# A fused attention and two-layer feed-forward kernel: the first token block takes its weights in two parts, with the second block between them

## The chip, the cores and the metric

The kernel runs on one core of a Trainium2 chip. The metric is device time in microseconds of one execution; the median over the runs is compared. Engines are called as in the profile: PE (matrix products; PEld its weight loads), DVE (vector), ACT (scalar), POOL, and SP, whose queue issues the DMAs. Each engine works through its own instructions in order.

## What is computed

```python
# r, k, v, w: (4, 8, 768, 48); attention is a recurrence over the sequence
cur = einsum('bhd,bhe->bhde', u * k[t], v[t])
y[t] = einsum('bhd,bhde->bhe', r[t], state + cur)
state = w[t][..., None] * state + einsum('bhd,bhe->bhde', k[t], v[t])
# then two feed-forward layers over 3072 tokens, 384 -> 2048 -> 384 each
h = x @ w_in;  g = where(h >= 1, h, where(h <= -1, 0, (h + 1)**2 / 4));  x = g @ w_out
h = x @ w2_in; g = where(h > 0, h, exp(min(h, 0)) - 1);                  out = g @ w2_out
```

The feed-forward weights arrive as 64-bit floats; the kernel converts them to 32 bits itself.

## The kernel before, in words

Attention is done in 24 steps (`attention`, stages of `QuotientAttention.stages`), each for 128 tokens. The 3072 tokens form six blocks of 512, four steps each. A block and a layer make a job: jobs 0 to 5 are the first layer on blocks 0 to 5, jobs 6 to 11 the second layer. A job runs 16 slots, one for each 128 hidden units, f = 0 to 15. A slot (job, f) is gemm1 (line 172, nine matmuls of 512 columns; operands are split in a high and a low part, so three products replace one), the activation (`first`, `second`; lines 183 to 192), the split of its result (`split`, 217 on ACT and 218 on DVE) and gemm2 (line 227, nine matmuls, which add into three PSUM banks y over all 16 slots; the first six need ACT's half of the split only). After slot 15 `store_y` copies y out (line 234 on ACT) and stores it.

Weight f (`weight_stages`) is loaded (111), taken apart on ACT (118, 119), converted on DVE (125 to 130: `last`), and cut in high and low part by ACT (135) and DVE (136: `parts`). The 16 weights of the first layer stay in SBUF for all its jobs, in `wpool` (line 75); raw weights of the first half are loaded into places that later hold weights of the second half, raw weights 10 and 12 into the second buffer of x (`RAW_X`).

An attention step has seven stages: `decays` (438 to 442, DVE), `operands`, `scores`, `masked` (479), `placed`, `out`, `stored`. Steps 0 to 3 write x of block 0 straight to SBUF (`x_act`, 425 and 426); the others store to DRAM (`out_act`, 343), from where `load_x` (158) and `split_x` (164, 165) fetch the block's x one job ahead.

The order of the work is written out by hand: `at(tick, rank, fn)` files each piece under a tick, and at the end (798 to 800) all pieces are emitted by tick and rank. Slot (ji, f) starts at tick t0 + 16 ji + f, with gemm1 at this tick, activation one tick later, the split two and gemm2 three ticks later; t0 is 20. `START` and `AT1` place the attention steps of blocks 0 and 1, `AT` those of the later blocks, `WSTART` the weights; `RANK_W`, `RANK_A` and `RANK_S` order the pieces within a tick. In block 0 weight f is due at tick t0 + f, so one weight for each slot (line 782). The framework may move a piece a little ahead where an engine would else stand idle. While steps 0 to 3 run, idle matmuls on zeros (`warm`, 151) are put on PE.

After block 5's attention `swap` frees its buffers, a second set of y banks is opened and the second layer's weights are converted (lines 791 to 797).

Of the kernel before, what the change touches and what calls it, by code (L numbers as in the profile page):

```python
# [9 lines left out]
F32 = mybir.dt.float32  # L10
F32R = mybir.dt.float32r
I32 = mybir.dt.int32
# [17 lines left out]
NB = max(BLOCKS) * TS  # L30


START = [0, 4, 8, 12]
AT1 = [-4, 0, 3, 7]
AT = [-6, 0, 4, 7]
T0 = 2
WSTART = [15, 16, 18, 24, 25, 27, 23, 23, 27, 34, 29, 35, 34, 36, 40, 45]
W2, W2_STEP = 4, 1.65
W_AHEAD, X_AHEAD, X_SPLIT = 1, 2, 1

RANK_W = [[148, 62, -48], [96, 102, -10]]
RANK_A = [[80, 126, 173, 72, 35, 21, 37], [72, 103, 199, 65, -3, 0, 8]]
RANK_S = [[-12, 45, 56, 52, -26], [-15, 37, 46, 56, -7]]

ON_ACT = {0: 0b0110101101101101, 5: 0b1111111011111101, 6: 0b1000100000011110}
TOK_POOL = {(6, 1), (7, 1), (7, 2), (6, 0)} | {(s, 2) for s in range(8, NSTEP)}
RAW_X = [10, 12]
NMORE = 5

WARM = [[3, 3, 3, 3, 3, 3, 3], [1, 2, 0, 3, 2, 2, 2], [2, 1, 4, 3, 4, 1, 2], [3, 2, 2, 1, 2, 3, 2]]  # L50
# [13 lines left out]
class Moe:  # L64


    def __init__(self, tc, ctx):
        self.tc, self.nc = tc, tc.nc
        nc = self.nc

        def pool(name, bufs, **kw):
            return ctx.enter_context(tc.tile_pool(name=name, bufs=bufs, **kw))

        const = pool("const", 1)
        self.wpool = [pool("wpool0", NF // 2), pool("wpool1", NF // 2)]
        self.xp = pool("xp", 2)
        self.ep = pool("ep", 2)
        self.gp = pool("gp", 2)
        self.ph = pool("ph", 2, space=PSUM)
        self.py = [pool("py", 1, space=PSUM)]  # L80
        self.one = const.tile([P, 1], F32, name="one")
        nc.gpsimd.memset(self.one, 1.0)
        self.half = const.tile([P, 1], F32, name="half")
        nc.gpsimd.memset(self.half, 0.5)
        self.zero = const.tile([P, P], mybir.dt.bfloat16, name="zero")
        nc.gpsimd.memset(self.zero, 0.0)
# [4 lines left out]

    def place(self, f):

        return self.wpool[f // (NF // 2)], "w"

    def new_raw(self, pool=None, tag="w_raw"):
        return (pool or self.wraw).tile([P, 2 * DM, 2], I32, name="w_raw", tag=tag)
# [52 lines left out]
        for _ in range(n):  # L150
            self.nc.tensor.matmul(y, self.zero, free_ap(self.zero, 0, P, 0, [[0, 512]]), start=True, stop=True)

    def new_x(self):
        return self.xp.tile([P, 2, 3, NB], F32R, name="x_hl")

    def load_x(self, src, t0, n):
        x = self.new_x()
        self.nc.sync.dma_start(x[:, 1, :, :n].bitcast(F32), src.rearrange("(k p) t -> p k t", p=P)[:, :, t0:t0 + n])
        return x

# [66 lines left out]
                self.nc.tensor.matmul(y[d][:, :n], w[:, a, DM + d * P:DM + (d + 1) * P], g[:, b, :n],  # L227
                                      start=first and j == 0, stop=last and j == 2)

    def store_y(self, y, dst, t0, n):  # L230
        nc = self.nc
        for d in range(3):
            o = self.ep.tile([P, NB], F32, name="y_o")
            nc.scalar.copy(o[:, :n], y[d][:, :n])  # L234
            nc.sync.dma_start(dst[d * P:(d + 1) * P, t0:t0 + n], o[:, :n])

    def run(self, jobs, weights):

        for m, src, dst, t, n in jobs:
            x = self.load_x(src, t, n)  # L240
            self.split_x(x, n)
            y = [self.py[0].tile([P, 512], F32, name=f"y{d}") for d in range(3)]
            for f in range(NF):
                h = self.gemm1(weights[(m, f)], x, n)
                first, second, g = self.act1(h, n, False) if m == 0 else self.act2(h, n, False)
                first()
                second()
                self.gemm2(weights[(m, f)], self.split(g, n), y, n, f == 0, f == NF - 1)
            self.store_y(y, dst, t, n)
# [412 lines left out]
def rwkv_moe_moe(ctx: ExitStack, tc: tile.TileContext, io, out):  # L662
# [7 lines left out]
    with ExitStack() as mctx:  # L670
# [12 lines left out]
        xs, ys, hs, gs, weights = {}, {}, {}, {}, {}  # L683

        def raw(m, f):
            if m == 0 and f < NF // 2:
                return moe.new_raw(*moe.place(NF // 2))
            if m == 0 and f in RAW_X:
                if f == RAW_X[0]:
                    xs["raw"] = moe.xp.tile([P, len(RAW_X), 2 * DM, 2], I32, name="x_raw", tag="x_hl")  # L690
                return xs["raw"][:, RAW_X.index(f)]
            return moe.new_raw()

        def weight(tick, m, f, place):
            st = {}
# [33 lines left out]
        def slot(tick, ji, f):  # L729
# [15 lines left out]
                gs[k] = moe.split(hs.pop(k)[2], n)  # L745

            def g2():
                if f == 0 and ji:
                    ys[ji] = [moe.py[ji % len(moe.py)].tile([P, 512], F32, name=f"y{d}") for d in range(3)]
                moe.gemm2(weights[(m, f)], gs.pop(k), ys[ji], n, f == 0, f == NF - 1)  # L750
                if f == NF - 1:
                    moe.store_y(ys.pop(ji), dst, t, n)

            at(tick, RANK_S[int(ji > 0)][0], g1)
            at(tick + 1, RANK_S[int(ji > 0)][1], first)
# [4 lines left out]
        def load_x(tick, ji):  # L760
            _, src, _, t, n = jobs[ji]

            def load():
                xs[ji] = moe.load_x(src, t, n)

            at(tick, 90, load)
            at(tick + X_SPLIT, 65, lambda: moe.split_x(xs[ji], n))
# [9 lines left out]
        for s in range(BLOCKS[0]):  # L777
            attention(START[s], s)
        t0 = START[BLOCKS[0] - 1] + 6 + T0
        at(0, 0, lambda: xs.update({0: moe.new_x()}))  # L780
        for f in range(NF):
            weight(min(WSTART[f], t0 + f - 3), 0, f, lambda f=f: moe.place(f))
        for ji in range(2 * nb):
            for f in range(NF):
                slot(t0 + ji * NF + f, ji, f)
            if ji:
                load_x(t0 + ji * NF - X_AHEAD, ji)
            if ji and ji < nb:
                for i in range(BLOCKS[ji]):
                    attention(t0 + (ji - 1) * NF + (AT1 if ji == 1 else AT)[i], steps[ji] + i)  # L790
        end = t0 + (nb - 2) * NF + AT[-1] + 7
        at(end, 99, swap)
        for f in range(NF):
# [104 lines left out]
```

## Time and profile before

| | us |
|---|---|
| runs | 953.8, 953.16, 948.65 (median 953.16) |
| profiled execution, its own time | 949.87 |
| its span, first to last instruction | 948.1 |
| PE busy | 913.5 (96%) |
| DVE busy | 623.5 (66%) |
| ACT busy | 588.3 (62%) |

Busy time is a mean over stages with different limits. The row of 40 slices shows where an engine is full, and windows of single stretches show how much it stands idle there. Matmuls overlap, so a slot's cost on PE is read from the distance between starts and not from single durations; DVE instructions overlap a little as well.

### The profile page before, as it was taken

The numbers are of one execution on the slowest core, as the hardware profiler recorded it, in microseconds if no ns is written. First come the engines' busy times: TensorE is split into PE (matmuls) and PEld (weight loads), VectorE is DVE, ScalarE is ACT, GpSimd is POOL, SyncE is SP. The second block draws the span as 40 slices with busy tenths as digits, with TensorE's granted clock in tenths as the row PEclk, the third lists the DMA queues.
The fourth block names the chain that finished last, engine by engine and source line by source line (L and its number), as shares of the span: only waits on it lengthen the run. The fifth ranks groups of instructions, "written<-read, shape, count | busy, mean of one in ns | idle before, by whom it ended". The sixth has DMA issues, their size and how long they took to land. (4 is left out here: it accounts for less than half of the span.)

```text
span 948.1 us, 15178 instructions
## 1 busy us (share of the span) xinstructions
PE 913.5 (96%) x5981; PEld 735.1 (78%) x5985; DVE 623.5 (66%) x923; ACT 588.3 (62%) x948; POOL 28.3 (3%) x41
## 2 busy tenths in 40 slices
PE   9787989999999999999999999999999999999996
PEld 4565767788888888888888888888888888888885
DVE  8999899856556755754399995555555545555552
ACT  5798767978878887877699973333433432433322
POOL 1000100000000000000000000000000000000000
PEclk9879999999999999999999999999999999999999
DMA  7876443434233422520274420100100101000001
GB/s 221 303 237 206 141 124 112 132 111 129 69 101 107 129 92 91 159 89 22 55 291 139 165 68 1 34 34 1 55 12 1 67 1 34 34 1 1 34 1 37
DMA packets 41184, 86.25 MB, mean 91 GB/s; under 512 B 5008, under 2 KB 18448, under 8 KB 41104
## 3 DMA queue, kind: packets, MB, share of 16 engines
q1 hardware_dynamic: 41104, 85.20, 27.9%
q8 instruction: 49, 0.80, 0.3%
q14 instruction: 31, 0.25, 0.1%
HBM read 71.81 MB, written 13.37 MB: 90 GB/s over the span
## 5 line engine op out<-in xcount | busy, mean ns | idle before, releaser
L172 PE MATMUL h<-x_hl,w_hl 128*128 128x512 f32 x1728 | 436.8, 397 | 10.9 <-DVE e_g L192 6.4
L227 PE MATMUL y<-g_hl,w_hl 128*128 128x512 f32 x1728 | 427.2, 391 | 4.2 <-DVE g_hl L218 4.2
L172 PEld LDWEIGHTS h<-x_hl,w_hl 128*128 128x128 f32 x1728 | 323.4, 190 | 81.2 <-DVE e_g L192 6.3
L227 PEld LDWEIGHTS y<-g_hl,w_hl 128*128 128x128 f32 x1728 | 324.0, 188 | 72.0 <-DVE g_hl L218 4.8
L218 DVE TENSOR_TENSOR g_hl<-e_g,g_hl 128x512 fp32r<-128x512 f32 x192 | 135.6, 706 | 74.2 <-ACT g_hl L217 73.8
L207 ACT ACTIVATE e_g<-e_g 128x512 f32<-128x512 f32 x90 | 56.9, 632 | 169.2 <-DVE e_g L206 169.2
L217 ACT CAST g_hl<-e_g 128x512 fp32r<-128x512 f32 x192 | 118.5, 617 | 54.0 <-PE y L227 48.6
L210 DVE SCALAR_TENSOR_TENSOR e_g<-e_g,h 128x512 f32<-128x512 f32 x96 | 66.1, 688 | 69.1 <-ACT e_g L207 65.0
L192 DVE TENSOR_TENSOR e_g<-h,e_g 128x512 f32<-128x512 f32 x96 | 65.9, 687 | 59.5 <-ACT e_g L185 59.2
L206 DVE TENSOR_SCALAR e_g<-h 128x512 f32<-128x512 f32 x90 | 62.2, 691 | 56.0 <-PE h L172 55.9
L183 ACT ACTIVATE e_g<-h,half 128x512 f32<-128x512 f32 x88 | 60.3, 685 | 34.7 <-PE h L172 32.0
L184 ACT ACTIVATE e_g<-e_g,one 128x512 f32<-128x512 f32 x88 | 63.8, 725 | 2.2
L185 ACT ACTIVATE e_g<-e_g 128x512 f32<-128x512 f32 x88 | 55.6, 632 | 1.4
L442 DVE TENSOR_TENSOR rk_sb<-rk_sb,w_sb 128x1024 f32<-128x1024 f32 x24 | 29.3, 1222 | 22.1 <-DMA rk_sb<-in_rkq 22.0
L465 PEld LDWEIGHTS sc<-tt,rk_sb 64*64 64x64 f32 x768 | 26.8, 140 | 9.0 <-issue 4.5
L136 DVE TENSOR_TENSOR w_hl<-w_z,w_hl 128x768 fp32r<-128x768 f32 x32 | 30.5, 954 | 3.2 <-ACT w_hl L135 3.1
L234 ACT COPY y_o<-y 128x512 f32<-128x512 f32 x36 | 20.4, 581 | 18.9 <-PE y L227 12.5
L465 PE MATMUL sc<-tt,rk_sb 64*64 64x64 f32 x768 | 31.1, 228 | 1.1 <-ACT tt L310 0.4
L360 PEld LDWEIGHTS ds<-vk_sb,rk_sb 64*64 64x64 f32 x704 | 20.6, 134 | 13.9 <-issue 7.5
L438 DVE TENSOR_TENSOR_SCAN w_sb<-w_sb,start 128x520 f32<-128x520 f32 x24 | 29.7, 1236 | 2.3 <-DMA w_sb<-in_wq 2.3
L441 DVE TENSOR_TENSOR_SCAN w_sb<-w_sb,start 128x520 f32<-128x520 f32 x24 | 30.1, 1256 | 0.5
L135 ACT CAST w_hl<-w_z 128x768 fp32r<-128x768 f32 x32 | 26.6, 832 | 4.8 <-DVE w_z L130 4.7
(68 smaller groups left out, 601.2 us busy)
## 6 DMA issues: line engine op xcount, KB each, us to landing
w_raw<-in_w SPq DMA_DIRECT2D x30, 768.0 KB, 5.1
rk_sb<-in_rkq SPq DMA_DIRECT2D x24, 512.0 KB, 3.9
tok_sb<-in_tokq SPq DMA_DIRECT2D x24, 384.0 KB, 3.1
w_sb<-in_wq SPq DMA_DIRECT2D x24, 260.5 KB, 3.5
x2d<-y_o SPq DMA_DIRECT2D x18, 256.0 KB, 2.2
x_hl<-x2d SPq DMA_DIRECT2D x6, 768.0 KB, 4.5
out_y<-y_o SPq DMA_DIRECT2D x18, 256.0 KB, 2.0
vk_sb<-in_vkq SPq DMA_DIRECT2D x22, 192.0 KB, 4.0
```

The source lines that it names most:

```text
L172: self.nc.tensor.matmul(h[:, :n], w[:, a, k * P:(k + 1) * P], x[:, b, k, :n], start=i == 0, stop=i == 8)
L183: nc.scalar.activation(out=g, in_=h[:, :n], func=AF.Relu, bias=self.half, scale=-0.5)
L184: nc.scalar.activation(out=g, in_=g, func=AF.Relu, bias=self.one, scale=-1.0)
L185: nc.scalar.activation(out=g, in_=g, func=AF.Square)
L192: nc.vector.tensor_tensor(out=g, in0=h[:, :n], in1=g, op=ALU.max)
L206: nc.vector.tensor_scalar_min(g, h[:, :n], 0.0)
L207: nc.scalar.activation(out=g, in_=g, func=AF.Exp)
L210: nc.vector.scalar_tensor_tensor(out=g, in0=g, scalar=1.0, in1=h[:, :n], op0=ALU.subtract, op1=ALU.max)
L217: nc.scalar.copy(gh[:, 0, :n], g)
L218: nc.vector.tensor_tensor(out=gh[:, 1, :n], in0=g, in1=gh[:, 0, :n].bitcast(F32), op=ALU.subtract)
L227: self.nc.tensor.matmul(y[d][:, :n], w[:, a, DM + d * P:DM + (d + 1) * P], g[:, b, :n], start=first and j == 0, stop=last and j == 2)
L465: nc.tensor.matmul(ps[64 * hh:64 * hh + 64, u], c["rk"][q:q + 64, 0, NU - 1 - u], c["tt"][q:q + 64, hh, u], start=True, stop=True)
```

## The change

Block 0 (job 0) runs its slots 0 to 6, then job 1 runs all its 16 slots, then job 0 its slots 7 to 15 (`SPLIT`, `order`). After slot (0,6) y is copied out and stored in the rows of `x2d` that job 0 fills at the end anyway; `load_part` fetches it into a free raw weight buffer near the end of the second part, and after slot (0,15) `store_y` adds it on DVE instead of copying on ACT. The first slot stands at tick 29 instead of 20; the attention steps of block 1 start at ticks 16, 19, 22 and 26, those of block 2 at 37, 42, 46 and 49. Weights follow `WSTART` alone. Every weight place and both x buffers become pools of their own; raw weights 0 to 7, 10 and 11 lie in places of weights 8 to 15. The ranks, and the engine of some activations in jobs 5 and 6 (`ON_ACT`), are set anew.

```diff
@@ -30,21 +30,24 @@
 NB = max(BLOCKS) * TS
 
 
-START = [0, 4, 8, 12]
-AT1 = [-4, 0, 3, 7]
-AT = [-6, 0, 4, 7]
-T0 = 2
-WSTART = [15, 16, 18, 24, 25, 27, 23, 23, 27, 34, 29, 35, 34, 36, 40, 45]
+START = [0, 4, 9, 12]
+AT1 = [-13, -10, -7, -3]
+AT2 = [8, 13, 17, 20]
+AT = [-6, 0, 3, 6]
+T0 = 11
+WSTART = [21, 22, 20, 25, 24, 29, 33, 37, 37, 39, 37, 42, 44, 44, 46, 46]
 W2, W2_STEP = 4, 1.65
+X_POOL = [0, 1, 1] + [ji % 2 ^ 1 for ji in range(3, 12)]
 W_AHEAD, X_AHEAD, X_SPLIT = 1, 2, 1
 
-RANK_W = [[148, 62, -48], [96, 102, -10]]
-RANK_A = [[80, 126, 173, 72, 35, 21, 37], [72, 103, 199, 65, -3, 0, 8]]
-RANK_S = [[-12, 45, 56, 52, -26], [-15, 37, 46, 56, -7]]
-
-ON_ACT = {0: 0b0110101101101101, 5: 0b1111111011111101, 6: 0b1000100000011110}
+RANK_W = [[148, 62, -48], [103, 102, -10]]
+RANK_A = [[80, 146, 173, 72, 35, 21, 85], [39, 103, 199, 65, -3, 0, -18]]
+RANK_S = [[-38, 51, 56, -11, -26], [-4, 37, 46, 56, -7]]
+
+ON_ACT = {0: 27501, 5: 28415, 6: 34836}
 TOK_POOL = {(6, 1), (7, 1), (7, 2), (6, 0)} | {(s, 2) for s in range(8, NSTEP)}
-RAW_X = [10, 12]
+RAW = {f: NF // 2 + f for f in range(NF // 2)} | {10: 14, 11: 15}
+SPLIT = 7
 NMORE = 5
 
 WARM = [[3, 3, 3, 3, 3, 3, 3], [1, 2, 0, 3, 2, 2, 2], [2, 1, 4, 3, 4, 1, 2], [3, 2, 2, 1, 2, 3, 2]]
@@ -72,8 +75,8 @@
             return ctx.enter_context(tc.tile_pool(name=name, bufs=bufs, **kw))
 
         const = pool("const", 1)
-        self.wpool = [pool("wpool0", NF // 2), pool("wpool1", NF // 2)]
-        self.xp = pool("xp", 2)
+        self.wpool = [pool(f"wpool{f}", 1) for f in range(NF)]
+        self.xp = [pool("xp0", 1), pool("xp1", 1)]
         self.ep = pool("ep", 2)
         self.gp = pool("gp", 2)
         self.ph = pool("ph", 2, space=PSUM)
@@ -91,7 +94,7 @@
 
     def place(self, f):
 
-        return self.wpool[f // (NF // 2)], "w"
+        return self.wpool[f], "w"
 
     def new_raw(self, pool=None, tag="w_raw"):
         return (pool or self.wraw).tile([P, 2 * DM, 2], I32, name="w_raw", tag=tag)
@@ -150,11 +153,11 @@
         for _ in range(n):
             self.nc.tensor.matmul(y, self.zero, free_ap(self.zero, 0, P, 0, [[0, 512]]), start=True, stop=True)
 
-    def new_x(self):
-        return self.xp.tile([P, 2, 3, NB], F32R, name="x_hl")
-
-    def load_x(self, src, t0, n):
-        x = self.new_x()
+    def new_x(self, i):
+        return self.xp[i].tile([P, 2, 3, NB], F32R, name="x_hl")
+
+    def load_x(self, src, t0, n, i):
+        x = self.new_x(i)
         self.nc.sync.dma_start(x[:, 1, :, :n].bitcast(F32), src.rearrange("(k p) t -> p k t", p=P)[:, :, t0:t0 + n])
         return x
 
@@ -227,17 +230,20 @@
                 self.nc.tensor.matmul(y[d][:, :n], w[:, a, DM + d * P:DM + (d + 1) * P], g[:, b, :n],
                                       start=first and j == 0, stop=last and j == 2)
 
-    def store_y(self, y, dst, t0, n):
+    def store_y(self, y, dst, t0, n, part=None):
         nc = self.nc
         for d in range(3):
             o = self.ep.tile([P, NB], F32, name="y_o")
-            nc.scalar.copy(o[:, :n], y[d][:, :n])
+            if part is None:
+                nc.scalar.copy(o[:, :n], y[d][:, :n])
+            else:
+                nc.vector.tensor_add(o[:, :n], y[d][:, :n], part[:, d, :n])
             nc.sync.dma_start(dst[d * P:(d + 1) * P, t0:t0 + n], o[:, :n])
 
     def run(self, jobs, weights):
 
-        for m, src, dst, t, n in jobs:
-            x = self.load_x(src, t, n)
+        for i, (m, src, dst, t, n) in enumerate(jobs):
+            x = self.load_x(src, t, n, i % 2)
             self.split_x(x, n)
             y = [self.py[0].tile([P, 512], F32, name=f"y{d}") for d in range(3)]
             for f in range(NF):
@@ -683,13 +689,7 @@
         xs, ys, hs, gs, weights = {}, {}, {}, {}, {}
 
         def raw(m, f):
-            if m == 0 and f < NF // 2:
-                return moe.new_raw(*moe.place(NF // 2))
-            if m == 0 and f in RAW_X:
-                if f == RAW_X[0]:
-                    xs["raw"] = moe.xp.tile([P, len(RAW_X), 2 * DM, 2], I32, name="x_raw", tag="x_hl")
-                return xs["raw"][:, RAW_X.index(f)]
-            return moe.new_raw()
+            return moe.new_raw(*moe.place(RAW[f])) if m == 0 and f in RAW else moe.new_raw()
 
         def weight(tick, m, f, place):
             st = {}
@@ -745,11 +745,12 @@
                 gs[k] = moe.split(hs.pop(k)[2], n)
 
             def g2():
-                if f == 0 and ji:
+                begin, end = f == 0 or k == (0, SPLIT), f == NF - 1 or k == (0, SPLIT - 1)
+                if begin and k != (0, 0):
                     ys[ji] = [moe.py[ji % len(moe.py)].tile([P, 512], F32, name=f"y{d}") for d in range(3)]
-                moe.gemm2(weights[(m, f)], gs.pop(k), ys[ji], n, f == 0, f == NF - 1)
-                if f == NF - 1:
-                    moe.store_y(ys.pop(ji), dst, t, n)
+                moe.gemm2(weights[(m, f)], gs.pop(k), ys[ji], n, begin, end)
+                if end:
+                    moe.store_y(ys.pop(ji), dst, t, n, first_half.get("part") if k == (0, NF - 1) else None)
 
             at(tick, RANK_S[int(ji > 0)][0], g1)
             at(tick + 1, RANK_S[int(ji > 0)][1], first)
@@ -761,7 +762,7 @@
             _, src, _, t, n = jobs[ji]
 
             def load():
-                xs[ji] = moe.load_x(src, t, n)
+                xs[ji] = moe.load_x(src, t, n, X_POOL[ji])
 
             at(tick, 90, load)
             at(tick + X_SPLIT, 65, lambda: moe.split_x(xs[ji], n))
@@ -777,17 +778,30 @@
         for s in range(BLOCKS[0]):
             attention(START[s], s)
         t0 = START[BLOCKS[0] - 1] + 6 + T0
-        at(0, 0, lambda: xs.update({0: moe.new_x()}))
+        at(0, 0, lambda: xs.update({0: moe.new_x(X_POOL[0])}))
+
+
+        def load_part():
+            n = jobs[0][4]
+            p = first_half["part"] = moe.wraw.tile([P, 3, NB], F32, name="y_part", tag="w_raw")
+            nc.sync.dma_start(p[:, :, :n], x2d.rearrange("(k p) t -> p k t", p=P)[:, :, :n])
+
+        order = [(0, f) for f in range(SPLIT)] + [(1, f) for f in range(NF)] + [(0, f) for f in range(SPLIT, NF)]
+        order += [(ji, f) for ji in range(2, 2 * nb) for f in range(NF)]
+        first_half = {}
+        begins = {ji: t0 + order.index((ji, 0)) for ji in range(2 * nb)}
+        at(t0 + 2 * NF, 91, load_part)
         for f in range(NF):
-            weight(min(WSTART[f], t0 + f - 3), 0, f, lambda f=f: moe.place(f))
-        for ji in range(2 * nb):
-            for f in range(NF):
-                slot(t0 + ji * NF + f, ji, f)
-            if ji:
-                load_x(t0 + ji * NF - X_AHEAD, ji)
-            if ji and ji < nb:
+            weight(WSTART[f], 0, f, lambda f=f: moe.place(f))
+        for i, (ji, f) in enumerate(order):
+            slot(t0 + i, ji, f)
+        for ji in range(1, 2 * nb):
+            load_x(begins[ji] - X_AHEAD, ji)
+            if ji < nb:
+                ticks = [t0 + a for a in (AT1 if ji == 1 else AT2)] if ji < 3 else [begins[ji - 1] + a for a in AT]
+                assert ticks[-1] + 6 <= begins[ji] - X_AHEAD and RANK_A[1][6] < 90
                 for i in range(BLOCKS[ji]):
-                    attention(t0 + (ji - 1) * NF + (AT1 if ji == 1 else AT)[i], steps[ji] + i)
+                    attention(ticks[i], steps[ji] + i)
         end = t0 + (nb - 2) * NF + AT[-1] + 7
         at(end, 99, swap)
         for f in range(NF):
```

## Rows read from the trace of the kernel before

**Rows 1.** The page, busy tenths in 40 slices: PE, DVE, granted clock.

```profile
PE   9787989999999999999999999999999999999996
...
DVE  8999899856556755754399995555555545555552
...
PEclk9879999999999999999999999999999999999999
```

**Rows 2.** Windows: busy us (x instructions) of PE, PEld, DVE, ACT, POOL; clock, DMA.

```profile
0.00:66.00 66.00, 53.63 (x758) 34.38 (x762) 59.20 (x93) 46.47 (x76) 3.46 (x20) 0.87 0.79 255
0.00:156.30 156.30, 131.33 (x1355) 92.49 (x1360) 145.24 (x222) 119.93 (x190) 10.76 (x25) 0.91 0.62 203
4.30:151.10 146.80, 122.90 (x1299) 87.13 (x1301) 139.08 (x213) 113.02 (x180) 8.09 (x9) 0.91 0.63 204
150.00:190.00 40.00, 38.64 (x285) 31.04 (x284) 35.56 (x52) 33.63 (x58) 2.32 (x1) 1.00 0.34 107
```

**Rows 3.** Groups by line on DVE, 0 to 156.3 us, first and last of 24.

```profile
L136 DVE TENSOR_TENSOR w_hl<-w_z,w_hl 128x768 fp32r<-128x768 f32 x16 | 15.3, 953 | 2.9 <-ACT w_hl L135 2.9
L128 DVE SCALAR_TENSOR_TENSOR w_z<-w_raw,w_z 128x768 int32<-128x768 int32 x14 | 14.0, 1008 | 0.0
L130 DVE CUSTOM_DVE_ANT_0 w_z<-w_raw,w_z 128x1536 uint16<-128x1536 uint16 x14 | 13.4, 966 | 0.0
...
L218 DVE TENSOR_TENSOR g_hl<-e_g,g_hl 128x512 fp32r<-128x512 f32 x14 | 10.4, 744 | 0.0
L192 DVE TENSOR_TENSOR e_g<-h,e_g 128x512 f32<-128x512 f32 x15 | 10.1, 682 | 0.0
L126 DVE TENSOR_SCALAR w_z<-w_z 128x768 int32<-128x768 int32 x16 | 8.7, 551 | 0.0
L125 DVE TENSOR_SCALAR w_z<-w_z 128x768 f32<-128x768 f32 x16 | 8.7, 551 | 1.4 <-ACT w_z L118 1.4
...
L165 DVE TENSOR_TENSOR x_hl<-x_hl 128x1536 fp32r<-128x1536 f32 x1 | 1.8, 1752 | 0.0
L283 DVE MEMSET av<- 128x512 f32 x1 | 0.5, 485 | 0.9 <-PEq L887 0.9
```

**Rows 4.** Timeline of PE: start, us, line, operation, count, idle time before.

```profile
93.15 1.65 PE L227 MATMUL y<-g_hl,w_hl 128*128 128x512 f32 x3 [3.35 <-DVE g_hl L218]
94.92 3.89 PE L172 MATMUL h<-x_hl,w_hl 128*128 128x512 f32 x9
...
100.69 2.20 PE L172 MATMUL h<-x_hl,w_hl 128*128 128x512 f32 x9
```

**Rows 5.** Timeline of PE: gemm2 of slot (0,12), and the last matmuls.

```profile
151.10 1.65 PE L227 MATMUL y<-g_hl,w_hl 128*128 128x512 f32 x6
...
153.72 0.96 PE L227 MATMUL y<-g_hl,w_hl 128*128 128x512 f32 x3
...
931.49 8.32 PE L227 MATMUL y<-g_hl,w_hl 128*128 128x512 f32 x36
```

**Rows 6.** Timeline of PE: gemm1 of slots (2,0), (3,0), (6,8), (7,0).

```profile
237.64 2.33 PE L172 MATMUL h<-x_hl,w_hl 128*128 128x512 f32 x9
...
318.92 2.33 PE L172 MATMUL h<-x_hl,w_hl 128*128 128x512 f32 x9
...
574.49 2.20 PE L172 MATMUL h<-x_hl,w_hl 128*128 128x512 f32 x9
...
607.13 2.20 PE L172 MATMUL h<-x_hl,w_hl 128*128 128x512 f32 x9
```

**Rows 7.** Timeline of ACT: output copy of attention step 11, block 2's last.

```profile
222.69 0.58 ACT L343 COPY a_sb<-av 128x512 f32<-128x512 f32 x1
```

**Rows 8.** The page: the y copy on ACT; the x load of the second layer.

```profile
L234 ACT COPY y_o<-y 128x512 f32<-128x512 f32 x36 | 20.4, 581 | 18.9 <-PE y L227 12.5
...
x_hl<-x2d SPq DMA_DIRECT2D x6, 768.0 KB, 4.5
```

## The prediction

> **What bounds the kernel now.** I read the busy tenths in 40 slices first [rows 1]: from about 190 us PE is at 9 in every slice but the last, at the full granted clock, while in the first eight slices DVE is at 8 or 9 and PE falls to 7. So there are two regimes, and only the first can change much: after it the time is a fixed amount of PE work. The windows [rows 2] give its size: between 4.3 and 151.1 us DVE is busy for 139.1 of 146.8 us, so it stands idle 7.7 us, and by 66 us only some 2.5 us of that has passed (66 less 4.3 less 59.2). DVE bounds the start.
>
> The end is then the largest value, over the slots, of: time at which DVE has done all that is queued up to this slot's `split`, plus the PE work that is then still left. I make this sum for the kernel before, to get its error, and repeat it for the new order.
>
> *Prices on DVE.* Durations overlap a little: the 24 groups of [rows 3] (the first and the last stand there) add up to 162.3 us, on 145.2 us of busy time in the same stretch [rows 2], so each duration counts 0.89. One weight (L125, L126, L130, L128, L136) is 4.03 x 0.89 = 3.6 us, 57.4 us for sixteen. A slot's `second` is 0.61 us on the ACT form (twice that on the other), a `split` 0.66, the split of a loaded x 1.56. The stretch holds 9 attention steps; 145.2 less 57.4 (weights), 21.4 (20 instructions of `second`, 14 splits) and 4.0 (x, `x_act` and the memset) leaves 62.4 us, so 6.95 us a step.
>
> *Prices on PE.* Eight slots of the second half take 32.64 us [rows 6], so 4.08 a slot, 2.04 a gemm. A block that also carries four attention steps takes 81.28 us against 65.28, so 4.0 us a step; the two steps that end a sequence lack about 1.9 each.
>
> *The sum for before.* Its tightest slot is (0,12). In plan order DVE has by its split 9 steps, 16 weights, 18 halves of `second`, 13 splits and `x_act`: 62.4 + 57.4 + 11.0 + 8.6 + 2.0 = 141.4 us. With the start at 4.3 and 7.7 idle: 153.4. The trace has the last three matmuls of that slot, the ones that need DVE's half of the split, at 153.72 [rows 5]. PE work left there: 179 gemm2 and 177 gemm1 and a third of one, 726.9 us, and 15 steps less 3.8, 56.2: 783.1. The last matmul ends at 931.49 + 8.32 = 939.8 [rows 5], which is 786.1 later. So 3.0 us are lost afterwards, and the sum stands. From PE's end to the reported time of this execution (949.87, span 948.1) there are 10.1 us more, which the change doesn't touch.
>
> **The change part by part.** *The order.* The first slot moves from tick 20 to 29, behind three attention steps of block 1 and most of the fourth, which move ahead (16, 19, 22, 26 instead of 16, 20, 23, 27 while slots are interleaved no more). Block 0 then takes seven weights, block 1 all sixteen, block 0 the other nine. A weight is thus due once per slot only for the first seven; weight 7 is due 14 slots after the first and weight 15 is due 22 slots after it. No multiplication is added. PE does nothing but attention until the first slot, and is to be fed without gaps from then on.
>
> *First bound, the first slot (0,0).* DVE has before its split 8 steps (55.6), `x_act` (2.0), six weights (2, 0, 1, 4, 3, 5: 21.5) and one `second` and `split` (1.3): 80.3 us. Start 4.3, idle time in proportion (2.5 x 80.3 / 59.2 = 3.4): 88.0 us. PE then has left 192 gemm2 less two thirds of one and 189 gemm1, 775.9, and 16 steps less 3.8 and an output of the eighth, 61.3: 837.2. With the 3.0 lost as before: 928.2.
>
> *The clock.* Until there PE is mostly idle. What that does: after the gap of 3.35 us that ended at 93.15 one gemm took 3.89 us, at a granted clock of a half, the next ones 2.20 [rows 4]; 1.7 us for a fall, say 2.5 with the matmuls beside it. In the kernel before this lay in DVE's shadow; now it lies on PE's path. First bound: 930.7.
>
> *Second bound, (1,11).* Here the weights of the second half and block 2's attention have all been queued: 10 whole steps (69.5) and 1.3 of steps 10 and 11 (9.0), 16 weights (57.4), 22 halves of `second` (13.4), 19 splits (12.6), x of block 1 and `x_act` (3.5): 165.4 us. Start 4.3, idle in proportion (7.7 x 165.4 / 139.1 = 9.1): 178.8. PE left: 174 gemm2 less two thirds, 171 gemm1, 702.4; 13 steps less 3.8 and half of step 10, 50.5: 752.9. Plus 3.0: 934.7. This is the larger, and so the forecast: 5.1 us less than 939.8. At (1,1), where weights 7, 8 and 10 stand together, the same sum gives about 930.
>
> *What it costs besides.* The partial sum: three more y copies on ACT of 0.58 each [rows 8], and three stores. ACT is off the path here. Behind the stores on SP's queue stand loads of weights and of v; they wait at most until the copies are done, some 2 us, and a weight is loaded one tick (about 4 us) ahead; taken at nothing, 2 us at most. The bank of y is freed once more than before; gemm1 of another slot runs in between, so nothing, at most one copy (0.6). Reloading the sum is a DMA of the size and source of an x load, 4.5 us [rows 8], issued two ticks ahead: hidden, 0 to 4.5 (it would hold gemm2 of (2,0)). The add of a PSUM tile to an SBUF tile is not in the trace; the nearest row is L192, 0.68 us [rows 3], three of them against three ACT copies of 0.58; gemm2 of (2,0) waits for them behind what DVE has queued. DVE has some 30 us of slack there, so I take nothing, 0 to 2 us. Together 0, at most 9.
>
> *x of block 1* goes through DRAM. In the trace 15 us pass from the output copy at 222.69 [rows 7] to the first gemm1 at 237.64 [rows 6]. In the new order step 7's `masked` leaves DVE at about 84 us, its copy follows at about 87, x is there at 102; PE wants it nine gemms and 2.3 us of attention after 88, at about 109. Seven us of cover; none lost.
>
> *Raw buffers, pools, ranks.* Raw weights 10 and 11 move out of x's second buffer, so that x of block 1 can be loaded while they are in use: nothing, and its cover is in the paragraph above. New ranks, `ON_ACT` of jobs 5 and 6 and `AT` move work in a stretch where PE has no gap at all [rows 1]: 0, between -1 and +2.
>
> **The sum.** 934.7 + 10.1 = 944.8 against this execution's 949.87, 5.1 us less. The median of the runs is 953.16; the same difference gives 948.1.
>
> **The rivals.** *Tighter overlap.* If DVE idles no more than by the first 66 us (2.5 of 61.7, so 7 by (1,11)), the second bound falls to 932.3, and the first (930.7, or 928.2 without a fall of the clock) is near: 2 to 4 us better than forecast, 944 to 946, and 941.5 if only the first bound without a fall is left. For it: the attention steps have no slots between them. Against: PE and DVE are both full from 88 to 180 us, and any mismatch costs.
>
> *No difference.* The two chains now have the same length, and what one waits is no longer hidden by the other. From 150 to 190 us, where both were full before, PE was busy 38.6 of 40 us [rows 2]; that 3.5% on 90 us is 3 us, and with the upper costs above (partial sum, y bank, reload) up to 6: 951 to 954.
>
> *Slower: DVE starves before the first slot.* The place is the stretch from 35 to 88 us, where steps 4 to 7 must follow each other every three ticks through single buffers (token tile, v, scores) and two PSUM banks, with no slot work to fill in. Every us that DVE idles there moves the first slot and the end by one. I have allowed 3.4 us in the whole start, and the first bound is 4 us below the second; it decides from about 7.5 us of idle time on, and passes the kernel before from about 12.5. Were DVE busy for 70% of these 53 us, 16 us idle, 12.6 more than allowed: the end at 943.3, 3.5 us later than before, so 956.7, and 960.7 at 62%. Against: in the first three slices DVE runs at 8 and 9 tenths with attention alone [rows 1].
>
> *The clock falls again and again.* By the granted clock and the gemm of 3.89 us, one fall costs 1.7 us [rows 4]. If each later gap of PE (weights 7, 8, 10; the second bound) brings one, five falls add 8.5 to 928.2: 936.7, so 950.1. The Trainium skill, "TensorE: Matmul & The Clock Gate", section "Why this matters for your kernels", advises against idle gaps between bursts of matmuls, since the clock then drops to half rate; by it the long idle start would speak against this change. The trace agrees that gaps do this, and shows no fall once PE is full.
>
> **How the numbers follow.** Forecast 0.45 (a little over half of it under 948.4, the bound of the next sentence, so 0.26 faster and 0.19 same), tighter overlap 0.24 (faster), no difference 0.15, the clock 0.04 (both same), starved start 0.12 (slower). About 0.5%, 4.8 us, is what a measurement of this kernel can tell from no change. Faster 0.50, same 0.38, slower 0.12. The range from 940.5 to 957 takes in all but the far part of the starved start.
>
> **What would show it.** First gemm2 at 86 to 90 us; PE at 9 tenths from there on, with the DVE row still at 9 until 180; gemm2 of (1,11) near 179; PE's last matmul near 935; no wait of PE on `y_part` or on the loaded x of block 1. Wrong would be: a first gemm2 after 95, gaps of PE between 100 and 180 that add up to more than 8 us, or the granted clock at a half in more than one stretch after 90 us.

## The result, and the profile after

The changed kernel takes 942.31 us (median of 5 runs, 941.46 to 942.85), the kernel before beside it 952.76 (5 runs, 948.65 to 953.8): 10.4 us less, a ratio of 0.9897 with an interval of 0.9874 to 0.9919. The forecast was 948.1, 5.1 us less: the direction held and the time lies in the range of 940.5 to 957, but the gain is twice the forecast one.

| us | before | forecast | after |
|---|---|---|---|
| median of the runs | 953.16, with the later runs 952.76 | 948.1 | 942.31 |
| profiled execution, its own time | 949.87 | 944.8 | 942.46 |
| its span | 948.1 | | 940.6 |
| first gemm2 of slot (0,0) starts | | 86 to 90 | 89.31 |
| DVE's half of the split of (0,0) ends | | 88.0 | 90.92 |
| DVE's half of the split of (1,11) ends | | 178.8 | 174.22 |
| gemm2 of (1,11) starts | | near 179 | 175.57 |
| PE's last matmul ends | 939.8 | 934.7 | 932.4 |

The page of after, busy tenths and granted clock in 40 slices of 23.5 us, answers to [rows 1]:

```profile
PE   9767999999999999999999999999999999999996
...
DVE  8999999976566667643499995554554555555452
...
PEclk9958999999999999999999999999999999999998
```

PE now has its weak slices all at the start: the second to the fourth. From the fifth slice (94 us) on it is at 9 and at the full clock up to the last, where before it fell under 9 here and there up to the sixth. DVE is at 9 to the eighth slice. The windows (busy us with the number of instructions for PE, PEld, DVE, ACT, POOL, then the clock and the DMA) answer to [rows 2]; the border is the first gemm2:

```profile
4.30:89.30 85.00, 65.92 (x987) 45.91 (x986) 79.20 (x124) 58.54 (x98) 4.58 (x7) 0.82 0.71 228
89.30:176.30 87.00, 86.63 (x597) 69.50 (x596) 86.78 (x128) 82.70 (x136) 7.17 (x4) 1.00 0.55 181
```

Up to the first gemm2 DVE idles 5.8 us; in the next 87 us it idles 0.2 and PE 0.4, both full at once for the length of 18 slots. The timeline of PE (start, us, line, operation, count, idle time before) at the first gemm2, at the ones of (1,11) and (2,0), and at the end:

```profile
79.76 1.09 PE L322 MATMUL ktp<-idt,rk_sb 128*128 128x128 f32 x4 [5.23 <-issue]
...
85.52 1.19 PE L175 MATMUL h<-x_hl,w_hl 128*128 128x512 f32 x4 [0.30 <-DVE e_g L195]
86.64 0.67 PE L366 MATMUL ds<-vk_sb,rk_sb 64*64 64x48 f32 x16
87.24 1.21 PE L175 MATMUL h<-x_hl,w_hl 128*128 128x512 f32 x4
88.38 0.67 PE L366 MATMUL ds<-vk_sb,rk_sb 64*64 64x48 f32 x16
88.98 0.50 PE L175 MATMUL h<-x_hl,w_hl 128*128 128x512 f32 x1
89.31 0.63 PE L230 MATMUL y<-g_hl,w_hl 128*128 128x512 f32 x2
...
175.57 2.20 PE L230 MATMUL y<-g_hl,w_hl 128*128 128x512 f32 x9
177.99 2.35 PE L175 MATMUL h<-x_hl,w_hl 128*128 128x512 f32 x9 [0.22 <-DVE e_g L195]
...
243.78 2.34 PE L230 MATMUL y<-g_hl,w_hl 128*128 128x512 f32 x9
...
926.12 6.28 PE L230 MATMUL y<-g_hl,w_hl 128*128 128x512 f32 x27
```

The last three matmuls of a gemm2 need DVE's half of the split. On DVE this half of slots (0,0) and (1,11) is:

```profile
90.24 0.68 DVE L221 TENSOR_TENSOR g_hl<-e_g,g_hl 128x512 fp32r<-128x512 f32 x1
...
173.56 0.66 DVE L221 TENSOR_TENSOR g_hl<-e_g,g_hl 128x512 fp32r<-128x512 f32 x1
```

So it ends at 90.92 and 174.22. PE comes to the last three matmuls of (0,0) at about 92.8 us, after a gemm1 that stands between, and to those of (1,11) at about 176.9, 2.7 us after DVE was done.

Where the gain lies is read at gemm2 of (2,0), the first of block 2. It starts at 243.78 us; before, it was this row:

```profile
253.83 2.20 PE L227 MATMUL y<-g_hl,w_hl 128*128 128x512 f32 x9
```

That is 10.1 us earlier, but with one gemm1 (2.0 us) less done by then. From there to the last matmul after takes 688.6 us, before 686.0, so apart from this gemm1 the rest is equal to 0.6 us: the gain arises before block 2, and the new ranks and `ON_ACT` bring nothing behind it. What the new ranks do in the first stretch was not tested by itself.

Between 90 and 200 us the waits of PE (us in total, times, longest) come down to one row, and neither `y_part` nor block 1's x is in it; the add of the partial sum (a group on DVE between 236 and 248 us) costs 0.69 us a piece:

```profile
PE h L175 <- DVE e_g L195: 0.5, 2, 0.3
```

```profile
L240 DVE TENSOR_TENSOR y_o<-y,y_part 128x512 f32<-128x512 f32 x3 | 2.1, 689 | 0.9 <-PE y L230 0.9
```

### The profile page after: what moved, and what is told of

It reads as the page before. It is cut to its first block, busy times and chain, and to the rows that moved or that the text cites. A ratio compares the mean times of both kernels' runs of the same rounds, so it can differ in the third digit from the quotient of the medians.

```text
span 940.6 us, 15005 instructions
## 1 busy us (share of the span) xinstructions
PE 911.7 (97%) x5985; PEld 736.7 (78%) x5985; DVE 634.1 (67%) x929; ACT 584.6 (62%) x944; POOL 29.0 (3%) x41
## 5 line engine op out<-in xcount | busy, mean ns | idle before, releaser
L175 PE MATMUL h<-x_hl,w_hl 128*128 128x512 f32 x1728 | 427.2, 391 | 1.7 <-ACT w_hl L138 0.8
L366 PE MATMUL ds<-vk_sb,rk_sb 64*64 64x48 f32 x704 | 24.4, 226 | 10.7 <-DVE st L372 6.6
L133 DVE CUSTOM_DVE_ANT_0 w_z<-w_raw,w_z 128x1536 uint16<-128x1536 uint16 x32 | 31.3, 977 | 0.5 <-ACT w_raw L122 0.2
L444 DVE TENSOR_TENSOR_SCAN w_sb<-w_sb,start 128x520 f32<-128x520 f32 x24 | 29.6, 1234 | 2.5 <-DMA w_sb<-in_wq 2.4
L464 POOL TENSOR_TENSOR a_sb<-eyef,z_sb 128x512 f32<-128x512 f32 x17 | 21.3, 1254 | 324.7 <-DMA xd<-a_sb 138.4
```

Of the source, the lines that this page charges most:

```text
L175: self.nc.tensor.matmul(h[:, :n], w[:, a, k * P:(k + 1) * P], x[:, b, k, :n], start=i == 0, stop=i == 8)
```

## The experiments

Three readings were to be told apart. **A:** PE's own chain from the first slot on sets the end, and DVE, by the distance between the ends of its splits and the matmuls that need them (2.5 us at (1,9) to (1,12)), has some 2.7 us to spare in the dense stretch. **B:** DVE's queue up to (1,11) sets the end, as the forecast had it. **C:** the granted clock at the head of the dense stretch is part of the chain. In the table, before is the median of runs of the kernel before that were measured beside the run; runs with the same number share them.

| run | us | before | ratio, interval |
|---|---|---|---|
| e0_after_again | 941.37 | 951.2 | 0.9897, 0.9849 to 0.9946 |
| e5_no_split | 958.21 | 951.2 | 1.0065, 1.004 to 1.0091 |
| e2_dve_early | 940.97 | 951.2 | 0.9891, 0.9843 to 0.994 |
| e4_dve_mid_8 | 947.79 | 951.2 | 0.9963, 0.9944 to 0.9983 |
| e3b_cut_mid_3 | 943.49 | 951.64 | 0.9901, 0.987 to 0.9932 |
| e4b_cut_mid_6 | 945.11 | 951.64 | 0.9921, 0.9898 to 0.9944 |
| e2b_cut_early | 949.51 | 951.64 | 0.9975, 0.996 to 0.9991 |
| e6_warm | 945.61 | 951.1 | 0.9936, 0.9916 to 0.9956 |
| e10_cut_early_warm | 945.17 | 951.1 | 0.9932, 0.9909 to 0.9955 |
| e7_pool | 947.95 | 951.1 | 0.9962, 0.9945 to 0.9978 |
| e8_no_part | 941.35 | 951.1 | 0.9889, 0.9856 to 0.9923 |

**The changed kernel again (e0), and without the split (e5).** e0 has no edit. e5 keeps the late first slot and all else, but runs block 0 through in one piece, with a weight for each slot:

```diff
-WSTART = [21, 22, 20, 25, 24, 29, 33, 37, 37, 39, 37, 42, 44, 44, 46, 46]
+WSTART = [21, 22, 20, 25, 24, 29, 32, 33, 34, 35, 36, 37, 38, 39, 40, 41]
-SPLIT = 7
+SPLIT = NF
-        at(t0 + 2 * NF, 91, load_part)
```

> The changed kernel itself, as the reference for the runs beside it. Theory A (PE is the chain from the first slot on, and DVE has slack behind it) and theory B (the DVE queue up to slot (1,11) still sets the end, as the prediction had it) both expect 942 us and a span near 940.5.

> The late start without the split: the first slot at tick 29 and block 1's attention ahead of it as in the changed kernel, but block 0 takes all sixteen weights in one go, one tick apart, and no partial sum is stored. If the gain comes from sharing seven weights between two blocks, this loses it: the DVE queue up to slot (0,12) plus the PE work left is then 10 us longer than the tightest sum of the changed kernel, so 952 us or more, with gaps of PE between 100 and 160 us. The rival, that the gain comes from pulling block 1's attention ahead of the slots alone, expects 942 to 944 here.

e0 repeats the result. e5 is 16.8 us slower than e0, and 7.0 slower than the kernel before. Its window over the dense stretch, and three lines of its timeline in it:

```profile
89.00:176.00 87.00, 77.55 (x477) 59.99 (x476) 83.50 (x123) 69.50 (x108) 3.31 (x3) 0.94 0.45 145
...
152.92 1.22 DVE L448 TENSOR_TENSOR rk_sb<-rk_sb,w_sb 128x1024 f32<-128x1024 f32 x1
...
154.24 0.87 PE L322 MATMUL ktp<-idt,rk_sb 128*128 128x128 f32 x3 [5.53 <-issue]
154.88 3.68 PE L175 MATMUL h<-x_hl,w_hl 128*128 128x512 f32 x9
```

PE stands idle for 9.5 of 87 us, against 0.4 in after, and with a gap of 5.5 us comes a fall of the clock, in which one gemm takes 3.68 us. The profile names no releaser for that gap ("issue"), but the piece that ends it, `ktp`, reads `rk_sb`, and DVE finishes that at 154.14, 0.1 us before: DVE, busy for 83.5 of the 87 us, has pieces of weights in front of it. So the gain hangs on the split: to start late, with block 1's attention ahead, is not what brings it, and with these settings loses time without the split. The ranks of e5 are those that were set for the split; how fast a late start without it could be made isn't known. The split is therefore worth 16.8 us over this start, and 10 us, with all that came with it, over the kernel before.

**More DVE work, as products on a scratch tile (e2, e4).** Four of them at ticks 24 to 27, before the first slot (e2; of its edit the lines that matter are shown), or eight at ticks 40 to 47, in the dense stretch (e4):

```diff
+        for tick in [24, 25, 26, 27]:
+            at(tick, 0, lambda: nc.vector.tensor_mul(moe.scr, moe.scr, moe.scr))
```

> Four extra DVE instructions of about 0.65 us on a scratch tile, filed at ticks 24 to 27, ahead of the first slot: 2.6 us more in the DVE queue before the first split. Theory A: the first gemm2 moves from 89.3 to about 92 us and the time rises by the same 2.6 us, to 945. Theory B: the queue up to (1,11) grows by 2.6 us as well, so also 945. A rise of less than 1.3 us would speak against both: the first slot would then hang on something other than the DVE queue.

> Eight extra DVE instructions of about 0.65 us on a scratch tile, filed at ticks 40 to 47, between the first slot and slot (1,11): 5.2 us more in that part of the DVE queue. Theory B: the end moves by all of it, 5.2 us, to about 947.5. Theory A: PE hides it as far as DVE has slack there; under 2 us, so 942 to 944, with no new gap of PE between 90 and 200 us or gaps that add up to less than 2 us.

Neither answers its question. Since these products depend on nothing, they were moved to where DVE stood idle at the start: in the traces they run from 1.3 to 4.8 us and from 1.3 to 10.5 us. e2 shows that some us of DVE work cost nothing that early, and nothing else. In e4 the order of the first slots changed as well (PE's second gemm2 starts at 99.15 us; about 92.8 in e0), and it took 947.79 us; what of that is the order and what the added work isn't separated. The next three runs repeat work that hangs on the weights and so can't move.

**DVE's half of cutting a weight, done again.** Three more pieces of 0.87 us each, 2.6 us, for weights 0 to 2 (e2b) or 11 to 13 (e3b), and six, 5.3 us, for 11 to 13 (e4b). The edit without the lines that set `cuts` for these weights:

```diff
-            nc.vector.tensor_tensor(out=w[:, 1], in0=z, in1=w[:, 0].bitcast(F32), op=ALU.subtract)
+            for _ in range(cuts):
+                nc.vector.tensor_tensor(out=w[:, 1], in0=z, in1=w[:, 0].bitcast(F32), op=ALU.subtract)
```

> DVE's half of cutting weights 11, 12 and 13 is done twice, 2.6 us more in the DVE queue between 145 and 156 us, ahead of slot (1,11). Theory B (DVE's queue up to (1,11) sets the end): plus 2.6 us, 944.0. Theory A (PE is the chain; the split of (1,11) is done 2.7 us before PE needs it, and at least 2.5 us before in its neighbours): within 0.5 us of 941.4.

> DVE's half of cutting weights 11, 12 and 13 is done three times, 5.3 us more in the DVE queue between 145 and 156 us. Theory B: plus 5.3 us, 946.7. Theory A: the first 2.7 us are hidden, so plus 2.6 us, 944.0, with a gap of PE of about this size near 175 us.

> DVE's half of cutting weights 0, 1 and 2 is done twice (same result), three instructions of 0.95 us, 2.6 us with their overlap, which can't move ahead of the weights and stand before the first split. Theory A and B: the first gemm2 and the end move by 2.6 us, to 944.0. If the time rises by less than 1.3 us, the first slot doesn't hang on the DVE queue.

First gemm2 and last matmuls of e3b (in e4b they start at 88.20 and 929.22):

```profile
89.34 0.63 PE L231 MATMUL y<-g_hl,w_hl 128*128 128x512 f32 x2
...
927.92 6.28 PE L231 MATMUL y<-g_hl,w_hl 128*128 128x512 f32 x27
```

From the first gemm2 to the end of the last matmul after takes 843.1 us and e0 842.9, e3b 844.9, e4b 847.3. So of 2.6 us some 1.9 arrive at the end, and of 5.3 some 4.3. By the medians it is 2.1 of 2.6 and 3.7 of 5.3, and e3b's four runs fall in two pairs (942.5 and 942.6, and twice 944.35, of which one is the profiled). So 0.5 to 1.6 us are hidden, not 2.7. A's slack falls by e3b, where it expected 941.4 and 943.49 came. B's 944.0 is near there, but in e4b the 945.11 lie between A's 944.0 and B's 946.7: neither is exact. The waits of PE in e3b between 90 and 200 us show where time is lost:

```profile
PE h L176 <- DVE e_g L196: 0.9, 2, 0.6
PE y L231 <- DVE g_hl L222: 0.6, 1, 0.6
```

PE waits for DVE 1.5 us, 0.5 in after. In both it waits twice at gemm1 for `second` (`e_g`), which reads h and so frees its PSUM bank (h has two); after does so at 177.99, where DVE's half of the split is 2.7 us early. So the room was read at the wrong place: at the split there are 2.7 us, at h's bank none. In the dense stretch DVE's queue and PE's own chain are level, to about 1 us.

e2b was the surprise: 2.6 us before the first slot cost 7 to 8 us (949.51 against 942.31 and 941.37), where both A and B expected 2.6. The profiled execution, at 951.61, is one of its longer ones. PE's timeline of e2b, from the gemm1 ahead of the first slot's gemm2 to that gemm2:

```profile
88.45 1.22 PE L176 MATMUL h<-x_hl,w_hl 128*128 128x512 f32 x2 [1.03 <-DVE e_g L196]
89.60 1.09 PE L367 MATMUL ds<-vk_sb,rk_sb 64*64 64x48 f32 x16
90.62 2.07 PE L176 MATMUL h<-x_hl,w_hl 128*128 128x512 f32 x4
92.62 1.09 PE L367 MATMUL ds<-vk_sb,rk_sb 64*64 64x48 f32 x16
93.65 1.65 PE L176 MATMUL h<-x_hl,w_hl 128*128 128x512 f32 x3
95.09 0.63 PE L231 MATMUL y<-g_hl,w_hl 128*128 128x512 f32 x1
```

In after the same piece begins at 85.52, 2.9 us earlier, about the added work. Then the nine matmuls take 4.94 us in place of 2.90, and the two groups `ds` 1.09 each in place of 0.67. That makes 2.9 + 2.0 + 0.8, and the first gemm2 is 5.8 us later; from it to the last matmul there are 3.8 us more (846.9). The window from 88 to 99 us shows the clock that goes with it (the number behind POOL's):

```profile
88.00:99.00 11.00, 10.55 (x76) 7.31 (x77) 7.77 (x13) 5.35 (x10) 0.69 (x1) 0.51 0.36 139
```

It was at its half level (1.2 of 2.4 GHz) from 81.8 to 98.9 us, though PE had hardly a gap from 88.45 on; in after from 77.8 to 84.6 only. DVE, which needs h from PE, is busy for only 7.8 of these 11 us. That raised C.

**Matmuls on zeros before the first slot.** e6 adds three after each stage of steps 4 to 7, as steps 0 to 3 have some; e10 does that and e2b's edit. The line that sets t0 only moves up and isn't shown:

```diff
                 if s < BLOCKS[0]:
                     at(tick + i, rank, lambda i=i: moe.warm(ys[0][0], WARM[s][i]))
+                elif s < 8 and tick + i < t0 + 1:
+                    at(tick + i, rank, lambda: moe.warm(ys[0][0], 3))
```

> The changed kernel with matmuls on zeros in attention steps 4 to 7 as well, three after each stage that stands before the first slot, so that PE has fewer gaps there and the granted clock stays up. Theory A: no change within 1 us (941 to 943), since in the changed kernel the last stretch at half clock ends at 84.6 us, before the first gemm2 at 89.3. Theory C (the clock at the start of the dense stretch is part of the chain): up to 1.7 us less, 940; if the matmuls on zeros hold up attention's own, up to 3 us more.

> The kernel with the first cuts of weights 0, 1 and 2 done twice, which took 949.5 us instead of the 944 expected, now with the same matmuls on zeros in steps 4 to 7. There the clock stayed at a half until 98.9 us, ten us into the dense stretch. Theory C (the loss beyond 2.6 us is the clock): the clock is up when the dense stretch begins, and the time comes to 944 to 945.5. Rival (the framework put the first slots in a worse order): the time stays within 1.5 us of 949.5.

On the kernel as it is the zeros lose 3.3 to 4.2 us, a little more than the 3 expected at most: the first gemm2 comes at 91.7, 2.4 us later, and from there to the end it takes 843.0 us as in after, so the loss lies before it. That the zeros hold up the attention fits this. With them, though, the three cuts cost nothing: e10 is level with e6, and 4.3 us faster than e2b. Its window from 88 to 99 us:

```profile
88.00:99.00 11.00, 10.49 (x97) 7.70 (x97) 9.71 (x16) 10.02 (x17) 0.33 (x1) 1.00 0.48 165
```

The clock is full here, with 97 matmuls in place of 76 for the same 10.5 us of PE's busy time, and DVE is busy for 9.7 us. So C is borne out for e2b: with the clock up, its slow matmuls are gone. It is not shown alone. The first gemm2, in pieces of 1, 1 and 7 matmuls in e2b, is in three pieces of 3 in e10, so the rival of another order isn't excluded; and that the cuts cost nothing in e10 may also be because the zeros delay the attention and so leave DVE room.

**Less DVE work before the first slot.** e7 puts the product that makes `a_sb` (L464, in the attention's stage `operands`) on POOL in steps 0 to 6 too, 4.3 us less on DVE:

```diff
-TOK_POOL = {(6, 1), (7, 1), (7, 2), (6, 0)} | {(s, 2) for s in range(8, NSTEP)}
+TOK_POOL = {(6, 1), (7, 1), (7, 2), (6, 0)} | {(s, 2) for s in range(NSTEP)}
```

> The product that places z on the diagonal moves from DVE to POOL in attention steps 0 to 6 as well: seven instructions of 0.61 us less in the DVE queue before the first slot, 4.3 us. If the first slot hangs on the DVE queue, the first gemm2 comes at about 85 us and the time falls by 3 to 4.3 us, to 938. If the longer product on POOL (1.6 us) holds up the step that follows it, DVE idles instead, and less than 1.5 us is gained or something is lost.

The first gemm2 came at 90.1, not earlier, and the kernel was 5.6 to 6.6 us slower. On POOL a piece takes 1.04 to 1.84 us, on DVE 0.67 to 0.69. From 4.3 to 89.3 us DVE is busy for 76.4 us instead of 79.2, and spends the room on waits such as these:

```profile
DVE st L372 <- PE ds L366: 3.0, 4, 1.9
...
DVE a_sb L485 <- POOL a_sb L464: 2.0, 2, 1.3
```

In after the first is 0.8 us and the second isn't there. So the first slot doesn't hang on the length of DVE's queue alone; by these waits the attention steps form a chain through PE, DVE and POOL of about the same length. Which link holds it at 89 us stays open: e2b lengthens DVE's part and delays it, e7 shortens that part and doesn't help. The clock differs too: it is at half for 10.2 us up to 89.2 here, for 6.8 us up to 84.6 in after; its share isn't separated. The profiled execution (945.48) is the shortest of ten, so some 2.5 us of the median's loss aren't in the trace at all.

**Without the partial sum's way back.** e8 neither loads nor adds it, so block 0's first layer lacks the first seven slots:

```diff
-                    moe.store_y(ys.pop(ji), dst, t, n, first_half.get("part") if k == (0, NF - 1) else None)
+                    moe.store_y(ys.pop(ji), dst, t, n, None)
-        at(t0 + 2 * NF, 91, load_part)
```

> The stored partial sum is not fetched and not added, so block 0's first layer lacks its first seven slots: y is copied out by ACT at the end of the second part, as for every other job. It prices the reload, the wait for it and the three adds on DVE. Theory of the prediction: hidden, so no change within 0.7 us. Rival: gemm2 of (2,0) waits for the adds, and 1 to 3 us are gained.

It took 941.35 us against e0's 941.37: the reload and the three adds cost nothing.

**The kernel before, profiled four more times.** The changed kernel's runs lie within 2 us (941.09 to 942.85 over nine); those of the kernel before went from 947.76 to 957.14. The profiled one, from which the forecast was worked out, was among the short ones.

> The kernel before, profiled a second time, since its executions lie between 948 and 957 us while those of the changed kernel lie within 1.5 us. Theory: the difference between its executions arises in its starved stretch up to 170 us, where PE's gaps make the granted clock fall, at other places in each execution; then the two profiles differ in where the clock is at a half and in PE's gaps before 170 us, and agree after 200 us to 0.5 us. Rival: the difference is spread over the whole span (memory, refresh, a slower clock throughout); then the stretch from 250 us to the end differs as well.

> The kernel before, profiled again. Of its executions the two profiled so far took 949.9 and 949.2 us, while the median is 951 to 953 and single ones reach 957. Theory C: a longer execution has more or longer stretches at half clock before 170 us (about 0.5 us of time for each us at half clock) and is later from there on by a constant; rival: it is later by an amount that grows over the span.

> As the run before it: the kernel before, profiled again. Theory C expects any time over 951 us to go with more time at half clock before 170 us; the rival expects the stretch from 250 us on to be longer.

> As the two runs before it: the kernel before, profiled again, with the same expectations.

They took 949.16 (e1), 952.64, 952.48 and 952.69 us (e11 to e13). Of e1, the window from 128 to 145 us, the gemm2 of slot (2,0) and the last matmuls:

```profile
128.00:145.00 17.00, 13.84 (x120) 10.59 (x119) 16.26 (x27) 11.80 (x20) 1.37 (x1) 0.90 0.56 190
...
253.10 2.20 PE L227 MATMUL y<-g_hl,w_hl 128*128 128x512 f32 x9
...
930.89 8.32 PE L227 MATMUL y<-g_hl,w_hl 128*128 128x512 f32 x36
```

And of e11:

```profile
128.00:145.00 17.00, 13.94 (x129) 10.19 (x127) 15.21 (x24) 10.00 (x17) 1.37 (x1) 0.80 0.51 168
...
256.51 1.75 PE L227 MATMUL y<-g_hl,w_hl 128*128 128x512 f32 x7
...
934.37 8.32 PE L227 MATMUL y<-g_hl,w_hl 128*128 128x512 f32 x36
```

From that gemm2 to the end of the last matmul both take 686.1 or 686.2 us, and the other three 686.0 or 686.1. The whole difference of 3.5 us arises before 254 us, where DVE bounds the kernel before. One part of it is visible: a mean clock of 0.90 over 17 us is 3.4 us at the half level, 0.80 is 6.8 us. From gemm2 of (0,8) to that of (0,10), which lie there, it is 17.5 us in the profile of before and 17.6 in e1, but 18.6 to 19.2 in e11 to e13: the longer fall goes with 1.0 to 1.7 us. In all, up to 200 us, the clock was at half for 27 and 24 us in the two short executions and about 31 in each of the three long ones. It was so for 31 us in after and 27 in e0 as well, though, all of it before the first gemm2; so what a fall costs depends on where it lies. The remaining 2 us were not traced to a place.

## Why the prediction was right in its direction and too small

**The first bound** was near: the first gemm2 starts at 89.31, within the 86 to 90 of the check. Its sum was for DVE's half of the split, 88.0, and this ended at 90.92: the work was right (80.8 us, forecast 80.3), the idle time 5.8 instead of 3.4. PE's work behind it was right too: from the last three matmuls of (0,0), at about 92.8, to the end it takes 839.6 us, forecast 837.2 and 3.0. The reason held only in part. It was a sum over DVE's queue, and e7 shows that a shorter queue doesn't bring the slot forward.

**The second bound** was the forecast, and it is the step that failed. DVE was to be done with the split of (1,11) at 178.8 us and was at 174.22. The term that was mis-sized above all is DVE's idle time "in proportion": 9.1 us were taken, and up to 174.22 it idles 6.0. The work was 163.9 us instead of 165.4. With these the same sum gives 174.2 + 752.9 + 3.0 = 930.1, where 934.7 was forecast and 932.4 measured, while the first bound, with the 90.9 us of the trace, gives 931.1. So the two bounds came out in the other order: (1,11) no longer sets the end, PE comes to its split 2.7 us after it is there, and idles from the first slot on for 0.4 us in 87. The idle time of [rows 2] had been taken as a property of DVE's work. Most of it stood after 66 us, where every weight was due in its slot; after the change DVE has a queue there, and of its 6.0 us 5.8 lie before the first gemm2 starts. The link was wrong as well: e3b and e4b show DVE's queue within about 1 us of deciding, but where PE touches it in after is h's bank, which the sum doesn't have. (Two small slips of the sum: 62.4 us over 9 steps are 6.93 a step, not 6.95; 13 steps less 3.8 and half of one are 50.2, not 50.5.)

**The clock's 2.5 us** on the first bound was an allowance for nothing in the kernel as it is: the clock falls at 77.8 and is full again at 84.6, before the first gemm1 of the dense stretch, and stays full to 934.5 us. That PE is mostly idle until there was wrong: from 4.3 to 89.3 us it is busy for 65.9 of 85. The allowance was right about the danger: in e2b, with 2.6 us of added work, the fall reached into the dense stretch, and they became 7 to 8.

**The costs taken at nothing** were nothing: e8 for the reload and the adds; no wait on `y_part`, on the bank of y or on block 1's x in the row of PE's waits.

**From PE's end to the time:** 10.1 us, measured 942.46 - 932.4 = 10.1.

**From the profile to the median** was the second step that failed, by 3.4 us. The same difference was subtracted from 953.16, as if the 3.3 us between the profiled execution and the median were a constant. They belong to the kernel before: its executions differ in the stretch up to 254 us, in part by how long the clock falls there, and that stretch is what the change rebuilds. Some 1.5 to 2 us of the 3.3 may be the chance of three runs: beside the experiments the kernel before has medians of 951.1 to 951.6 over 14 to 18 runs. The changed kernel's profiled execution (942.46) stands at its median (942.31). Together: 2.3 us from the second bound and 3.4 from the carrying over are the 5.7 or 5.8 between 948.1 and 942.31.

**The rivals.** Tighter overlap comes nearest: it assumed 7 us of idle time and an end of PE at 932.3, against 6.0 and 932.4; 932.3 + 10.1 would have been 942.4, and only the carrying over made 944 to 946 of it. That it is so near is in part luck: it was still the bound at (1,11), which with the measured terms is 930.1. No difference assumed 3 us of mismatch while both engines are full; PE lost 0.4 in 87. The starved start came in small: DVE idles 5.8 us where 3.4 were allowed and 7.5 would have decided; with the second bound lower, this is enough to make the first slot the later bound. Repeated falls of the clock between 100 and 180 us came in e5, where PE has gaps, and not in the change. The rule of the Trainium skill weighed there ("TensorE: Matmul & The Clock Gate", "Why this matters for your kernels") is to leave no idle gaps between bursts of matmuls, since the clock then drops. The trace of after agrees as to the drop, half level from 77.8 to 84.6 us in and after the gap of 5.23 us that ends at 79.76; it cost the change nothing that shows, since it ended before the dense stretch.

## What to carry to other kernels

Where one engine feeds another through a rate that it can't keep, reorder the work so that the same input serves twice before the next is due; here this was worth 16.8 us over the same start without it, and 10 us over the kernel before. Don't scale idle time with work: ask for each stretch what the engine waited for, and drop what the change removes. Subtract a forecast difference from the profiled execution's own time, and look whether the spread of the runs comes from the stretch that the change removes, because then the median can gain that as well. And ask of a bound which instruction really waits there: the split had 2.7 us of room, h's bank none.

## What was not expected of the hardware

A fall of the granted clock has a price that depends on what follows: in the kernel before the longer fall went with 1.0 to 1.7 us, in after a fall of 6.8 us ahead of the dense stretch cost nothing that shows, and in e2b, with the fall at the head of that stretch, 2.6 us of delay became 7 to 8. In e2b the clock stayed at half for 17.1 us, the last ten of them with PE almost without a gap; why it stayed isn't shown. And 18 executions of the kernel before, whose clock falls between its slots, differ by 9 us (947.76 to 957.14), while those of the changed one, whose clock doesn't fall in the dense work, differ by 1 to 2; that the falls make all of the difference isn't shown.
